# One quarter of the first weight matrix through SyncE's queue, with its cast on VectorE

## The chip, the cores and the metric

The kernel runs on one core of a Trainium2 chip. The metric is device time in microseconds (us) for one launch. A core has five engines that each run their own instruction list in order: TensorE (PE in the profile, its weight loads PEld), VectorE (DVE), ScalarE (ACT), GpSimd (POOL) and SyncE (SP). Transfers between the chip's memory and the core are issued by SyncE, ScalarE or GpSimd, and are then carried out by 16 DMA engines that all queues share.

## The reference

Two functions in a row. The first is a causal convolution with 7 taps over time, one set of taps for each of 8 groups of 24 channels; the second is a two-layer network with a Swish whose steepness is a parameter for each hidden column.

```python
w = exp(weight - max(weight)); w = w / (sum(w) + 1e-9)         # weight: [8, 7]
out = einsum('hk,bskhg->bshg', w, windows_of_7(x))              # x: [8, 4096, 192]
h = out.reshape(32768, 192) @ w_in                              # w_in: [192, 2048]
g = h * (1 / (1 + exp(-beta * h)))                              # beta: [2048]
return (g @ w_out).astype(float32)                              # w_out: [2048, 192]
```

All inputs and the output are float32 in memory; the kernel multiplies in bf16 (the convolution of the first tile in fp32r).

## The kernel before

**Tiling.** The 32,768 tokens are cut into two streams of 16,384 (`NS = 2`), which lie in the two halves of the partitions. The 192 channels are cut in three (`NK = 3`), so that 64 partitions hold one third for one stream. A step i takes n tokens of each stream: 128, 128, 256 for i = 0, 1, 2, then larger ones up to 512. In a step, the first product (`mm1`, with `ph` as its PSUM tile) makes 128 hidden columns at a time, ScalarE applies the Swish (Silu with a scale), and the second product (`mm2`, into `po`) is run for the step before.

**The start.** Steps 0 to 2 are run apart, by `mm1_pair(i, u)` for u = 0 to 7. Call one such call (i, u). It multiplies two sets of 128 columns at once, number u and number u + 8: one from each half of `w_in`, with stream-independent weights in the two halves of the partitions. So (0, 0) and (0, 1) need columns 0 to 256 of each half, (0, 2) and (0, 3) columns 256 to 512, (0, 4) and (0, 5) columns 512 to 768, and (0, 6) and (0, 7) columns 768 to 1024. `ph` has two buffers: (i, u) can't begin until ScalarE has finished the call two before.

Between these calls, `first_tile(i, u)` places by hand the convolution of the first 512 tokens of each stream, four blocks of 128. For a block b, `transpose_0` (TensorE, L215) turns x; `take_0` (L223) copies the result from PSUM into `xr`; `conv_0` (L229) applies the taps as matmuls with diagonal weights, eight in its first part and six in its second; `evac_0` (L240 on VectorE) scales the two results into the `xcp` tiles that `mm1_pair` reads. Blocks 0 and 1 are turned before (0, 0). Blocks 2 and 3 (numbers from 0) are turned together at (0, 3). Block 1's convolution lies at (0, 1) and (0, 2), block 2's at (0, 5) and (0, 6), block 3's at (1, 0) and (1, 1). `scale_w_out` (L273), sixteen calls on VectorE, multiplies the rows of `w_out` by 1/beta; the first `mm2` calls (L374), from (1, 2) on, need them.

**Loading.** `w_in` is float32 in memory and wanted as bf16. `load_w_in` (L113) uses GpSimd's queue, whose transfers convert the type on the way. That queue carries, in this order:

```python
    for f0, f1 in ((0, 256), (256, 640), (640, HF)):      # HF = 1024, half of w_in
        for s in range(NS):
            load_w_in(s, HF * s + f0, HF * s + f1)
        if f0 == 256:
            for b in range(2, NB):
                load_x0(b, nc.gpsimd)                     # blocks 2 and 3 of x
```

After these eight transfers come four of `w_out` (L157), two for the next blocks of x (`xb1`, L159), two more of x (L81), and four `copy_w_in` (L116), which put each half of `w_in` also into the other half of the partitions, for step 3 on. The program makes the ninth and each later transfer of this queue wait until the one eight places before it has landed.

SyncE's queue carries only the taps, block 0 of stream 0, beta and block 1 of x before it comes to the transposes of step 3. All instructions of an engine keep the order in which the program writes them (`pin`).

Of the kernel before, what the change touches and what calls it, by code (L numbers as in the profile page):

```python
# [10 lines left out]
FP32 = mybir.dt.float32  # L11
# [8 lines left out]
def kernel(  # L20
# [9 lines left out]
    nc = tc.nc  # L30
# [7 lines left out]
    NK = 3  # L38
    Q = D // NK
    NS = 2  # L40
# [3 lines left out]
    NB = TILE // 128  # L44

    def pin(ins):

        return tc.keep_in_program_order(ins)
# [4 lines left out]
    consts = ctx.enter_context(tc.tile_pool(name="consts", bufs=1))  # L53
# [23 lines left out]
    def load_x(j, s, b0=0, b1=NB, eng=None):  # L77
        if j not in xf_of:
            xf_of[j] = xf_pool.tile([128, NB, NS, D], FP32, name="xf")
        src = xs[s, TILE * j + 128 * b0:TILE * j + 128 * b1, :]  # L80
        pin((eng or nc.sync).dma_start(out=xf_of[j][:, b0:b1, s, :],  # L81
                                       in_=src.rearrange("(b p) d -> p b d", p=128)))

    def cast_x(j, s, b0=0, b1=NB, eng=None):
        if j not in xbf_of:
            xbf_of[j] = xbf_pool.tile([128, NB, NK, NS, Q], BF16, name="xb")
        pin((eng or nc.vector).tensor_copy(  # L87
            xbf_of[j][:, b0:b1, :, s, :].rearrange("p b k q -> p k b q"),
            xf_of[j][:, b0:b1, s, :].rearrange("p b (q k) -> p k b q", k=NK)))

    def new_xt(j):
        xt_of[j] = xt_pool.tile([128, NK, LEAD + TILE], BF16, name="xt")

    def transpose_x(j, b):
        if j not in xt_of:
            new_xt(j)
        c = LEAD + 128 * b
        pin(nc.sync.dma_start_transpose(
            out=xt_of[j][:, :, c:c + 128],
            in_=xbf_of[j][:, b, :, :, :].rearrange("p k s q -> p (k s q)")))  # L100


    w_in_s = consts.tile([128, NK, F], BF16, name="w_in_s")
    w_in_v = moe_w_in.rearrange("(q k) f -> q k f", k=NK)
# [4 lines left out]
    def half_of(s):  # L109
        return slice(64 * s, 64 * s + 64)  # L110

    def load_w_in(s, f0, f1):
        pin(nc.gpsimd.dma_start(out=w_in_s[half_of(s), :, f0:f1], in_=w_in_v[:, :, f0:f1]))  # L113

    def copy_w_in(s, f0, f1):
        pin(nc.gpsimd.dma_start(out=w_in_s[half_of(1 - s), :, f0:f1], in_=w_in_s[half_of(s), :, f0:f1]))  # L116
# [3 lines left out]
    xb0 = consts.tile([128, 2, NS, D], BF16, name="xb0")  # L120
# [7 lines left out]
    HF = F // 2  # L128

    def load_x0(b, eng):  # L130
        pin(eng.dma_start(out=x0[:, b, :, :] if b < 2 else xb0[:, b - 2, :, :],  # L131
                          in_=xs[:, 128 * b:128 * b + 128, :].rearrange("s p d -> p s d")))

    load_x0(1, nc.sync)

    one = consts.tile([128, 1], FP32, name="one")
    pin(nc.vector.memset(one, 1.0))
# [9 lines left out]
                                pattern=[[0, NS], [-1, H], [0, Q // H]], channel_multiplier=1))  # L147
    pin(nc.gpsimd.affine_select(out=ident, in_=ident, compare_op=ALU.not_equal, fill=1.0,  # L148
                                base=0, pattern=[[-1, 128]], channel_multiplier=1))
    for f0, f1 in ((0, 256), (256, 640), (640, HF)):  # L150
        for s in range(NS):
            load_w_in(s, HF * s + f0, HF * s + f1)
        if f0 == 256:
            for b in range(2, NB):
                load_x0(b, nc.gpsimd)
    for c in range(0, NF, 4):
        pin(nc.gpsimd.dma_start(out=w_out_f[:, c:c + 4, :], in_=w_out_v[:, c:c + 4, :]))  # L157
    for s in range(NS):
        pin(nc.gpsimd.dma_start(out=xb1[:, :, s, :],  # L159
                                in_=xs[s, TILE:TILE + 256, :].rearrange("(b p) d -> p b d", p=128)))  # L160
# [12 lines left out]
    def po_banks():  # L173
        return [po_bank(), po_bank()]
# [34 lines left out]
    def transpose_0(bank, src, b):  # L209

        bf = src.dtype == BF16
        t = (bank.bitcast(BF16) if bf else bank)[:, 0:NK * 128].rearrange("p (k t) -> p k t", k=NK)
        v = src[:, b, :, :].rearrange("p s d -> p (s d)").rearrange("p (m k) -> p k m", k=NK)
        for kk in range(NK):
            pin(nc.tensor.transpose(t[:, kk, :], v[:, kk, :], ident_b if bf else ident))  # L215
        return t

    def take_0(t, b, act=False):
        dst = xr[:, :, PAD + 128 * b:PAD + 128 * b + 128]
        if act:  # L220
            pin(nc.scalar.activation(dst, t, AF.Copy))
        else:
            pin(nc.vector.tensor_copy(dst, t))  # L223

    def conv_0(cv, b, k0=0, k1=K):

        for k in range(k0, k1):
            for s in range(NS):
                pin(nc.tensor.matmul(  # L229
                    cv[s][:, 0:NK * 128], diag[half_of(s), k, :, :].rearrange("p s q -> p (s q)"),  # L230
                    xr[half_of(s), :, 128 * b + k:128 * b + k + 128], start=(k == 0), stop=(k == K - 1)))

    def evac_0(cv, b, s, eng, k0=0, k1=NK):
        i, c = place[b]
        src = cv[s][:, 128 * k0:128 * k1].rearrange("p (k t) -> p k t", t=128)
        dst = xc_of[i][:, s, k0:k1, c:c + 128]
        if eng is nc.scalar:
            pin(nc.scalar.activation(dst, src, AF.Copy, scale=rsum))
        else:
            pin(eng.tensor_scalar_mul(dst, src, rsum))  # L240

    new_xt(0)
    pa = po_banks()
    pb = po_banks()
# [4 lines left out]
        make_diag(k)  # L249
    rsum = consts.tile([128, 1], FP32, name="rsum")  # L250
    pin(nc.vector.reciprocal(rsum, tsum))
    for f in range(0, HF, 512):
        for s in range(NS):
            copy_w_in(s, HF * s + f, HF * s + f + 512)
    pin(nc.scalar.activation(scrap, one, AF.Silu))
    b0 = [cv0[:, 0, :], pb[0]]
    conv_0(b0, 0)
# [6 lines left out]
    beta = consts.tile([128, NF], FP32, name="beta")  # L264
    pin(nc.vector.tensor_copy(beta, beta_ps))
    take_0(t1, 1)
    rbeta = consts.tile([128, NF], FP32, name="rbeta")
    pin(nc.vector.reciprocal(rbeta, beta))
    tapn = consts.tile([128, K], FP32, name="tapn")
# [2 lines left out]
    def scale_w_out(c):  # L272
        pin(nc.vector.tensor_scalar_mul(w_out_s[:, c, :], w_out_f[:, c, :], rbeta[:, c:c + 1]))  # L273
# [225 lines left out]
    def first_tile(i, u):  # L499
        if (i, u) == (0, 1):  # L500
            conv_0(pb, 1, 0, 4)
        elif (i, u) == (0, 2):
            conv_0(pb, 1, 4, K)
        elif (i, u) == (0, 3):
            t23 = [transpose_0(pa[b], xb0, b) for b in range(2)]
            for b in range(2):
                take_0(t23[b], 2 + b)
            for s in range(NS):
                evac_0(pb, 1, s, nc.vector)
        elif (i, u) == (0, 5):  # L510
            conv_0(pa, 2, 0, 4)
            for c in range(4):
                scale_w_out(c)
        elif (i, u) == (0, 6):
            conv_0(pa, 2, 4, K)
            for s in range(NS):
                evac_0(pa, 2, s, nc.vector)
            for c in range(4, 8):
                scale_w_out(c)
        elif (i, u) == (1, 0):  # L520
            conv_0(pb, 3, 0, 4)
        elif (i, u) == (1, 1):
            conv_0(pb, 3, 4, K)
            for s in range(NS):
                evac_0(pb, 3, s, nc.vector)
            for c in range(8, NF):
                scale_w_out(c)
        elif (i, u) == (1, 6):
            new_xt(1)
            ts_ = [transpose_0(pb[b], xb1, b) for b in range(2)]  # L530
            for b in range(2):
                pin(nc.vector.tensor_copy(xt_of[1][:, :, LEAD + 128 * b:LEAD + 128 * b + 128], ts_[b]))
            pin(nc.vector.tensor_copy(xt_of[0][:, :, TILE + LEAD - PAD:],
                                      xr[:, :, TILE:].bitcast(FP32)))
        elif (i, u) == (1, 7):
            for s in range(NS):
                cast_x(1, s, 2, NB)
            for b in range(2, NB):
                transpose_x(1, b)
            for j in (2, 3):  # L540
                for s in range(NS):
                    load_x(j, s)
# [69 lines left out]
```

## Time and profile before

| What | Value |
|---|---|
| Median of four runs | 686.74 us (686.05 to 687.60) |
| The profiled execution, its own time | 686.78 us |
| Its span in the profile | 684.9 us |
| TensorE busy | 679.4 us (99% of the span) |
| ScalarE busy, VectorE busy | 584.8 us (85%), 551.1 us (80%) |
| Granted TensorE clock | 1.00 |

The profiled execution's own time is 1.9 us over its span, and it is 0.04 us over the median. Times below are counted from the span's start. Spans of a busy TensorE are modelled at their end, and consecutive ones overlap; the starts of instructions are what the text reads. In a timeline line the first number is the start, the second the length of the merged piece, and the bracket at its end tells how long the engine was idle before it and what ended that.

### The profile page before, as it was taken

The numbers are of one execution on the slowest core, as the hardware profiler recorded it, in microseconds if no ns is written. First come the engines' busy times: TensorE is split into PE (matmuls) and PEld (weight loads), VectorE is DVE, ScalarE is ACT, GpSimd is POOL, SyncE is SP. The second block draws the span as 40 slices with busy tenths as digits, with TensorE's granted clock in tenths as the row PEclk, the third lists the DMA queues.
The fourth block names the chain that finished last, engine by engine and source line by source line (L and its number), as shares of the span: only waits on it lengthen the run. The fifth ranks groups of instructions, "written<-read, shape, count | busy, mean of one in ns | idle before, by whom it ended". The sixth has DMA issues, their size and how long they took to land.

```text
span 684.9 us, 27204 instructions
## 1 busy us (share of the span) xinstructions
PE 679.4 (99%) x12528; PEld 460.4 (67%) x12528; DVE 551.1 (80%) x886; ACT 584.8 (85%) x585; POOL 14.5 (2%) x26
## 2 busy tenths in 40 slices
PE   9999999999999999999999999999999999999998
PEld 6799887666666666666666666666666666666667
DVE  5999999999988889878889888889878889875112
ACT  7999999888888888888888888888888888888881
POOL 7000000000000000000000000000000000000000
PEclk9999999999999999999999999999999999999999
DMA  9752444344422444523444323344324443220223
GB/s 193 195 138 85 124 109 118 83 117 117 118 71 66 109 109 117 116 55 84 106 112 117 103 53 99 100 118 117 94 49 106 105 117 72 59 57 5 49 48 94
DMA packets 150418, 66.85 MB, mean 98 GB/s; under 512 B 113648, under 2 KB 149696, under 8 KB 150304
## 3 DMA queue, kind: packets, MB, share of 16 engines
q1 hardware_dynamic: 146992, 61.08, 34.9%
q0 software_dynamic: 3168, 3.93, 2.8%
q8 instruction: 98, 1.61, 1.0%
q14 instruction: 16, 0.13, 0.1%
q10 hardware_dynamic: 144, 0.10, 0.0%
HBM read 28.32 MB, written 25.17 MB: 78 GB/s over the span
## 4 chain that ended last, share of the span: by engine, by line
PE 97%; DMA 1%; POOL 1%; ACT 1%; issue 0%; DVE 0%; POOLq 0%
PE ph L342 47%; PE po L420 43%; PE po L374 4%; PE po L458 2%; PE ph L325 1%; DMA w_in_s<-in_moe_w_in_dram 1%; ACT g L329 1%; POOL w_in_s L113 0%; PE po L229 0%; ACT gp L329 0%; POOL xb L131 0%; PE po L215 0%; POOL sel L146 0%; DVE o_sp L380 0%; POOL ident L148 0%
## 5 line engine op out<-in xcount | busy, mean ns | idle before, releaser
L346 ACT ACTIVATE g<-ph,beta 128x1024 bf16<-128x1024 f32 (+2 forms) x528 | 558.1, 1062 | 80.4 <-PE ph L342 62.3
L342 PE MATMUL ph<-xc,w_in_s 64*64 64x512 bf16 (+3 forms) x5952 | 617.6, 369 | 0.3 <-ACT g L329 0.3
L420 PE MATMUL po<-g,w_out_s 64*64 64x512 bf16 (+1 forms) x5568 | 580.9, 373 | 0.0
L342 PEld LDWEIGHTS <-w_in_s 64*64 64x64 bf16 (+1 forms) x5952 | 274.9, 104 | 125.6 <-issue 0.5
L420 PEld LDWEIGHTS <-w_out_s 64*64 64x64 bf16 x5568 | 290.4, 118 | 84.3
L303 DVE SCALAR_TENSOR_TENSOR acc<-xt,tapn,acc 128x512 f32<-128x512 bf16 (+2 forms) x450 | 311.0, 759 | 0.9
L437 DVE STREAM_TRANSPOSE o_sb<-po 128x512 f32<-128x512 f32 (+1 forms) x87 | 76.1, 875 | 112.3 <-PE po L420 112.2
L303 DVE SCALAR_TENSOR_TENSOR xc<-xt,tapn,acc 128x512 bf16<-128x512 bf16 (+2 forms) x90 | 63.9, 760 | 0.2
L87 DVE CAST xb<-xf 128x768 bf16<-128x768 f32 (+1 forms) x62 | 48.7, 822 | 0.0
L301 DVE TENSOR_SCALAR acc<-xt,tapn 128x512 f32<-128x512 bf16 (+2 forms) x90 | 40.9, 485 | 1.1
L374 PE MATMUL po<-w_out_s,g 64*128 64x192 bf16 x512 | 32.6, 243 | 0.0
L374 PEld LDWEIGHTS <-g 64*128 64x128 bf16 x512 | 24.9, 94 | 1.6
L325 PE MATMUL ph<-xcp,w_in_s 64*128 64x256 bf16 (+1 forms) x144 | 15.1, 307 | 1.1 <-DMA w_in_s<-in_moe_w_in_dram 0.8
L380 DVE COPY o_sp<-po 128x192 f32<-128x192 f32 x28 | 9.0, 352 | 8.4 <-PE po L458 7.3
L329 ACT ACTIVATE gp<-ph,beta 128x256 bf16<-128x256 f32 x32 | 12.7, 476 | 1.9 <-PE ph L325 1.5
L458 PEld LDWEIGHTS <-g 128*128 128x128 bf16 x128 | 10.5, 98 | 0.4 <-issue 0.4
L458 PE MATMUL po<-w_out_s,g 128*128 128x192 bf16 x128 | 10.7, 247 | 0.0
L325 PEld LDWEIGHTS <-w_in_s 64*128 64x128 bf16 x144 | 6.8, 94 | 4.6 <-issue 1.6
L329 ACT ACTIVATE g<-ph,beta 128x512 bf16<-128x512 f32 x16 | 9.6, 692 | 0.1
L374 PE MATMUL po<-w_out_s,gp 64*128 64x192 bf16 x128 | 7.6, 243 | 0.0
L229 PE MATMUL po<-xr,diag 64*128 64x384 f32 x49 | 7.0, 362 | 0.0
L374 PEld LDWEIGHTS <-gp 64*128 64x128 bf16 x128 | 6.0, 94 | 1.6
(52 smaller groups left out, 57.3 us busy)
## 6 DMA issues: line engine op xcount, KB each, us to landing
xf<-in_x_dram SPq DMA_DIRECT2D x60, 384.0 KB, 4.1
out_dram<-o_sb SPq DMA_DIRECT2D x108, 192.0 KB, 4.6
xt<-xb SPq DMA_TRANSPOSE x122, 2.4
out_dram<-o_sp SPq DMA_DIRECT2D x10, 192.0 KB, 3.4
w_out_f<-in_moe_w_out_dram POOLq DMA_DIRECT2D x4, 384.0 KB, 7.6
out_dram<-o_sb SPq DMA_DIRECT2D x8, 144.0 KB, 4.3
w_in_s<-w_in_s POOLq DMA_DIRECT2D x4, 192.0 KB, 6.5
out_dram<-o_sp SPq DMA_DIRECT2D x8, 96.0 KB, 1.9
```

The source lines that it names most:

```text
L87: pin((eng or nc.vector).tensor_copy(xbf_of[j][:, b0:b1, :, s, :].rearrange("p b k q -> p k b q"), xf_of[j][:, b0:b1, s, :].rearrange("p b ...
L301: pin(nc.vector.tensor_scalar_mul(a, src, w))
L303: pin(nc.vector.scalar_tensor_tensor(out=xc_of[i][:, k0:k1, o:o + m] if k == K - 1 else a, in0=src, scalar=w, in1=a, op0=ALU.mult, op1=ALU ...
L325: pin(nc.tensor.matmul(ph[:, h, 0:NS * n], w_in_s[half_of(h), kk, ts(fcs[h], 128)], xc_of[i][half_of(h), :, kk, :], start=(kk == 0), stop= ...
L329: pin(nc.scalar.activation(g_at(i, fcs[h])[:, :, 0:n], ph[:, h, 0:NS * n].rearrange("p (s t) -> p s t", s=NS), AF.Silu, scale=beta[:, fcs[ ...
L342: pin(nc.tensor.matmul(ph[m0:m1, s, 0:n], w_in_s[half_of(s), kk, 128 * fc + m0:128 * fc + m1], xc_of[i][half_of(s), kk, 0:n], start=(kk == ...
L346: pin(nc.scalar.activation(g_at(i, fc)[:, :, 0:n], ph[:, :, 0:n], AF.Silu, scale=beta[:, fc:fc + 1]))
L374: pin(nc.tensor.matmul(po[q][:, 0:D], g_at(i, fc)[r, s, ts(b, 128)], w_out_s[r, fc, :], start=(phase == 0 and fc == 0), stop=(phase == 1 a ...
L380: pin(nc.vector.tensor_copy(dst, po[:, 0:D]))
L420: pin(nc.tensor.matmul(po_of[i, m][half_of(s), 0:n], w_out_s[half_of(r), fc, m:D:NM], g_at(i, fc)[half_of(r), s, 0:n], start=(first and fc ...
L437: pin(nc.vector.transpose(osb_of[i][:, 0:n // L, :, m], po_of[i, m][:, 0:n].rearrange("p (b l) -> p b l", l=L)))
L458: pin(nc.tensor.matmul(po[:, 0:D], g_at(i, fc)[:, s, ts(b, 128)], w_out_s[:, fc, :], start=(fc == 0), stop=(fc == NF - 1)))
```

## The change

The columns 256 to 512 of each half of `w_in` no longer go through GpSimd's queue. SyncE loads them as float32 into a new tile `w_in_f`, two transfers issued behind block 1 of x, and VectorE casts them into `w_in_s` in four copies of 64 partitions by 3 x 128 elements. These stand on VectorE between `take_0` of block 1 and the reciprocal of beta. The four `copy_w_in` are written behind the casts, and the two that hold those columns wait for them.

GpSimd's queue now carries columns 0 to 256, then 512 to 768, then block 2 of x, then columns 768 to 1024, then block 3 of x: again eight transfers before `w_out`. Block 3 of x is turned at (0, 7) in place of (0, 3), into another PSUM bank, and is taken by VectorE there, behind block 2's `evac_0`. The first eight `scale_w_out` follow it, where before four stood at (0, 5) and four at (0, 6).

```diff
     load_x0(1, nc.sync)
+    W0, W1 = 256, 512
+    w_in_f = consts.tile([128, NK, W1 - W0], FP32, name="w_in_f")
+    for s in range(NS):
+        pin(nc.sync.dma_start(out=w_in_f[half_of(s), :, :], in_=w_in_v[:, :, HF * s + W0:HF * s + W1]))
...
-    for f0, f1 in ((0, 256), (256, 640), (640, HF)):
+    for f0, f1, b in ((0, W0, None), (W1, 768, 2), (768, HF, 3)):
         for s in range(NS):
             load_w_in(s, HF * s + f0, HF * s + f1)
-        if f0 == 256:
-            for b in range(2, NB):
-                load_x0(b, nc.gpsimd)
+        if b:
+            load_x0(b, nc.gpsimd)
...
-    for f in range(0, HF, 512):
-        for s in range(NS):
-            copy_w_in(s, HF * s + f, HF * s + f + 512)
...
     take_0(t1, 1)
+    for f in range(0, W1 - W0, 128):
+        for s in range(NS):
+            w = HF * s + W0 + f
+            pin(nc.vector.tensor_copy(w_in_s[half_of(s), :, w:w + 128], w_in_f[half_of(s), :, f:f + 128]))
+    for f in range(0, HF, 512):
+        for s in range(NS):
+            copy_w_in(s, HF * s + f, HF * s + f + 512)
...
         elif (i, u) == (0, 3):
-            t23 = [transpose_0(pa[b], xb0, b) for b in range(2)]
-            for b in range(2):
-                take_0(t23[b], 2 + b)
+            take_0(transpose_0(pa[0], xb0, 0), 2)
             for s in range(NS):
                 evac_0(pb, 1, s, nc.vector)
         elif (i, u) == (0, 5):
             conv_0(pa, 2, 0, 4)
-            for c in range(4):
-                scale_w_out(c)
         elif (i, u) == (0, 6):
             conv_0(pa, 2, 4, K)
             for s in range(NS):
                 evac_0(pa, 2, s, nc.vector)
-            for c in range(4, 8):
+        elif (i, u) == (0, 7):
+            take_0(transpose_0(pb[0], xb0, 1), 3)
+            for c in range(8):
                 scale_w_out(c)
```

## The prediction

> **What bounds the kernel now.** I read the page's busy times and chain first, then the waits of the first 32 us, then the timeline of each engine there, then the transfers one by one.
>
> ```profile
> PE 679.4 (99%) x12528; PEld 460.4 (67%) x12528; DVE 551.1 (80%) x886; ACT 584.8 (85%) x585; POOL 14.5 (2%) x26
> ...
> PE 97%; DMA 1%; POOL 1%; ACT 1%; issue 0%; DVE 0%; POOLq 0%
> ...
> PEld L325 <- DMA w_in_s<-in_moe_w_in_dram: 1.3, 2, 1.0
> ...
> PE ph L325 <- DMA w_in_s<-in_moe_w_in_dram: 0.8, 1, 0.8
> ```
>
> TensorE is the bound; the change touches none of its work after step 2. What there is to win is the 1% of the chain that is a transfer of `w_in` (the waits' columns: total us, times, longest). It lies here:
>
> ```profile
> 10.28 0.52 PE L215 MATMUL po<-ident_b,xb 128*128 128x128 bf16 x6
> 10.73 0.81 PE L325 MATMUL ph<-xcp,w_in_s 64*128 64x256 bf16 x7
> 12.37 0.39 PE L325 MATMUL ph<-xcp,w_in_s 64*128 64x256 bf16 x4 [0.82 <-DMA w_in_s<-in_moe_w_in_dram]
> ...
> 13.32 0.50 PE L325 MATMUL ph<-xcp,w_in_s 64*128 64x256 bf16 x5
> ...
> 15.09 0.97 PE L229 MATMUL po<-xr,diag 64*128 64x384 f32 x8
> 15.90 0.51 PE L325 MATMUL ph<-xcp,w_in_s 64*128 64x256 bf16 x6
> ```
> ```profile
> 10.74 1.02 DVE L223 CAST xr<-po 128x384 fp32r<-128x384 bf16 x2 [2.18 <-PE po L215]
> ...
> 14.42 1.13 DVE L240 TENSOR_SCALAR xcp<-po,rsum 128x384 bf16<-128x384 f32 x2
> 15.47 0.99 DVE L273 TENSOR_SCALAR w_out_s<-w_out_f,rbeta 128x192 bf16<-128x192 f32 x4
> 16.97 1.14 DVE L240 TENSOR_SCALAR xcp<-po,rsum 128x384 bf16<-128x384 f32 x2 [0.51 <-PE po L229]
> ```
>
> In the first of these two timelines (TensorE, VectorE), 10.73 is (0, 4); its seventh matmul, at about 11.2, is the first of (0, 5), which then stops for columns 640 to 768 until 12.37. (0, 6) begins at 13.32, (1, 1) at 15.90. The reader is to note what VectorE does behind (0, 6): block 2's two `evac_0` from 14.42 to 15.47, and only then other work. Block 3 has by then long been taken, at 10.74 to 11.7.
>
> The transfers' own answers (issue start and time to landing) give: columns 0 to 256 landed at 5.7 and 6.3, columns 256 to 640 at 7.1 and 8.3, blocks 2 and 3 of x at 8.8 and 9.3, columns 640 to 1024 at 11.2 and 12.3. Two of those waits end the stall. From 4.2 us on, the DMA engines are full (2 to 12 us, 40 slices of 0.25 us):
>
> ```profile
> DMA  7680147879999999999899999998999888999999
> ```
>
> **The change, part by part.**
>
> *The stall at (0, 5).* Its columns now come in the queue's second piece, and (0, 6) needs the third, columns 768 to 1024. Ahead of that third piece lie 24 packets per engine less of `w_in`, one x block less, but 24 packets of SyncE's on the same engines. Packets counted in stretches of the transfers' view and divided by 16 engines: a converting packet of 512 B (columns 0 to 256) took an engine about 45 ns, of 768 B (the later pieces) 68 ns, of an x block about 32 ns, SyncE's 768 B ones about 35 ns, so I take 45 ns for its new 1,024 B ones. At about 5.1 us, 11 packets per engine of the first piece are left. Before: 11x45 + 24x68 + 32x32 + 24x68 = 4.8 us, so 9.9 on a mean engine, where 12.3 was the last landing: the slowest engine lags by 2.4. After: 11x45 + 24x45 + 16x32 + 24x45 + 24x45 (SyncE's) = 4.2 us, so 9.3, with the same lag 11.7 (estimates). (0, 5) can't begin before ScalarE is done with (0, 3), at 10.76 + 0.47 = 11.23; then 0.26 to its convolution and 0.81 for that (15.09 to 15.90) put (0, 6) at 12.30. So the piece is in time by 0.6 us, the stall is gone, and (0, 6) begins 1.02 us earlier (13.32 to 12.30).
>
> *What is late next: `take_0` of block 3.* It was at (0, 3); it now stands on VectorE behind block 2's two `evac_0`, and the convolution at (1, 0) waits for it. From the trace: (0, 6) to the first `evac_0` 1.10 us (13.32 to 14.42), the two 1.05 (14.42 to 15.47), the take 0.55 (one of 128x384 from PSUM, at 7.54), to the convolution 0.05, the convolution's first part 0.81, then (1, 1). That is 12.30 + 3.56 = 15.86, where (1, 1) began at 15.90. TensorE, which keeps its order, stands about 0.9 us at (1, 0) in place of (0, 5). Of 1.02 us won, 0.04 is left.
>
> *The three transposes taken out at (0, 3)* (0.23 us of TensorE) are put back at (0, 7), both beside a TensorE that waits for ScalarE or VectorE: nothing.
>
> *`scale_w_out`.* Its first eight calls at 0.247 us (0.99 for four) run from 14.96 (0.51 behind the take's start, as between the two takes at 10.74) to 16.94; block 3's `evac_0` was started by TensorE at 16.97. The first three are wanted by `mm2` at 17.1 and are done by 15.7. `w_out`'s first two transfers landed at 13.3 and 14.4. Nothing, by a margin of 0.03 us at block 3; behind that all stands as before, ScalarE being busy without a break from 17.33 to 31.75.
>
> *The four casts.* They fall into the 2.18 us in which VectorE waited (the bracket at 10.74), behind `take_0` of block 1, at 8.0. The nearest row is a cast of the same 384 elements, two in 0.90 us, one every 0.41:
>
> ```profile
> 21.11 0.90 DVE L87 CAST xb<-xf 128x384 bf16<-128x384 f32 x2
> ```
>
> At that price the first pair is done at 8.90 and the second at 9.7, in time for (0, 2) at 8.96 and (0, 3) at 9.84. [...] I take the row; the sum is the same by both, 0, as long as the data is there. The ends are 0 and, with the 0.49 of one cast alone, 0.15.
>
> *SyncE's two transfers.* Nothing else stands on SyncE's queue until 22 us, so no issue is delayed. They issue at about 2.5 and 2.9 and follow block 1 of x (3.9 us to landing, at 6.0). With its engines shared packet by packet, 24 x (45 + 45) ns from 5.1 gives 7.3 on a mean engine, and with the lag of 1 us that the second piece showed, 8.3 (estimate). The casts of stream-half 1 are wanted at 8.41. Ends: 7.0 (SyncE served first; no gain, the casts begin at 8.0), and 9.7 (GpSimd's packets served three to one). I take 0.1 us of delay at (0, 2), which goes to the end unchecked. The first piece shares too: 6.3 becomes about 6.9, wanted at 7.34; hidden by 0.4, and 0.3 of loss if SyncE goes first.
>
> *GpSimd's queue.* Eight transfers stand before `w_out` as before. The second of `xb1` and the next now wait for the third piece, the last x transfer for block 3: landings of about 11.7 and 12.4, where it waited until 12.6 before. Nothing. The `copy_w_in` issue at 13.6 and later, long after the casts.
>
> [...] The trace: seven scalings on VectorE, float32 from SBUF to SBUF, ran beside GpSimd's issue of two x transfers, which took 1.46 us; two more of that size, beside which VectorE was idle for the first half, took 1.46 too.
>
> ```profile
> 4.01 1.54 DVE L199 TENSOR_SCALAR diag<-ident,etap 128x128 fp32r<-128x128 f32 x7 [0.42 <-ACT etap L195]
> ...
> 4.32 1.46 POOL L131 DMA_DIRECT2D xb<-in_x_dram  x2
> ...
> 10.00 1.46 POOL L159 DMA_DIRECT2D xb<-in_x_dram  x2
> ```
>
> [...]
>
> **The sum.** Against the profiled execution's 686.78 us: -1.02 for the stall, +0.98 for the new wait, +0.1 for late `w_in_f`, 0 for the rest: 686.84, and 686.8 to 686.9 against the median of 686.74, which is 0.04 lower. I say 686.9.
>
> **The rivals.**
> 1. *The gain is kept.* If block 3 is taken in time, (1, 1) begins up to 1.0 us earlier, ScalarE's unbroken run with it, and the end too: 685.8. For it: ScalarE is fed from two buffers and may ride over part of the wait. Against: TensorE is in order, and the take stands behind two copies that can't begin until TensorE has finished block 2. `xb1`, which landed at about 19.5 for a use at 20.11, would also allow only half of it.
> 2. *`w_in_f` comes late (slower).* Place: the wait of VectorE's second cast, and (0, 2) behind it, one for one from a landing of 8.4 on. At 9.7 it costs 1.3, at 10.4 2.0: 688.1 to 688.8. For it: full engines, and a queue on which SyncE's packets came slowly at 3.4 to 4.0. Against: at 4.4 to 5.0 that queue moved more packets than GpSimd's.
> 3. *The load pieces of GpSimd's queue are not earlier.* If the lag of the slowest engine grows, the third piece lands at 12.8 or later and (0, 6) moves with it, and everything behind: +0.5 to +1.0, 687.3 to 687.8.
> 4. *The change doesn't do what it says*: the DMA engines are full, so a second queue moves the bytes no faster. True, but pieces are reordered, which is what the first part counts; it is part of the forecast.
>
> **How the numbers follow.** A measurement of this kernel can tell about 0.2% (1.37 us) from no change: faster is below 685.4, slower above 688.1. The forecast has 0.66, rival 1 0.10, rival 2 0.13, rival 3 0.11. The forecast and rival 3 lie within 0.2%, but for 0.05 of things that I don't see on the slow side. Rival 1 is within too, but for its far end (0.04). Two thirds of rival 2 are slower. That makes 0.04 faster, 0.82 within, 0.14 slower. The range from 685.9 to 688.1 leaves out the far half of rival 1 and the slower part.
>
> **What would show it.** Right: no wait of L325 for a transfer of `w_in` between 10 and 13; (0, 6) near 12.3; instead a wait of PE L229 for DVE `xr` of about 0.9 at 14.1; (1, 1) near 15.9; casts between 8.0 and 9.7 with no or little wait. Wrong: (1, 1) before 15.4 (rival 1); VectorE waiting for `w_in_f` at 8 and L325 for the casts (rival 2); a wait for `w_in_s` at (0, 6) (rival 3); or time that moves after 32 us, where I count nothing.

## The result and the profile after

| | before | changed |
|---|---|---|
| median | 686.73 us (61 runs, 685.90 to 687.60) | 687.95 us (41 runs, 687.18 to 688.64) |
| the profiled execution, and its span | 686.78, 684.9 us | 687.94, 686.2 us |

The ratio is 1.0018, with a 95% interval from 1.0014 to 1.0023: 1.2 us slower. The forecast was no measurable change, 686.9, with a range from 685.9 to 688.1, and it gave the late landing of `w_in_f` a chance of 0.13. The time lies in the range, but 1.1 us above the forecast's sum of 686.84. That it lies inside is luck: the range was wide, and what the traces below show is in good part that rival, not the sum.

The page and the waits of the first 32 us of the changed kernel (total us, times, longest):

```profile
PE 680.9 (99%) x12528; PEld 461.0 (67%) x12528; DVE 552.4 (81%) x890; ACT 584.6 (85%) x585; POOL 14.6 (2%) x26
...
PE 99%; ACT 1%; DVE 0%; issue 0%
```

```profile
PE po L232 <- DVE xr L226: 0.6, 1, 0.6
```

The transfer of `w_in` has gone from the chain and from TensorE's waits, and the wait of block 3's convolution for `take_0` has come, as forecast. But the timeline of TensorE shows a loss ahead of the first matmul that uses anything the change touches. These are matmuls of block 0's convolution in the changed kernel, and (0, 0), (0, 6), block 3's convolution and (1, 1):

```profile
5.93 0.52 PE L232 MATMUL ph<-xr,diag 64*128 64x384 f32 x1
...
6.25 0.52 PE L232 MATMUL ph<-xr,diag 64*128 64x384 f32 x1
...
8.72 0.85 PE L332 MATMUL ph<-xcp,w_in_s 64*128 64x256 bf16 x12
...
13.71 0.52 PE L332 MATMUL ph<-xcp,w_in_s 64*128 64x256 bf16 x6
...
16.45 0.98 PE L232 MATMUL po<-xr,diag 64*128 64x384 f32 x8 [0.62 <-DVE xr L226]
17.27 0.50 PE L332 MATMUL ph<-xcp,w_in_s 64*128 64x256 bf16 x6
```

The same place before, and (0, 0):

```profile
5.81 0.34 PE L229 MATMUL ph<-xr,diag 64*128 64x384 f32 x1
...
5.99 0.33 PE L229 MATMUL ph<-xr,diag 64*128 64x384 f32 x1
...
7.34 0.94 PE L325 MATMUL ph<-xcp,w_in_s 64*128 64x256 bf16 x12
```

The matmuls follow one another by 0.32 us after, by 0.18 before: TensorE ran at little more than half its speed (below: half speed). In the trace's record of its clock, full speed begins at 5.26 us in the first profiled execution of before and at 8.82 in this one; below, the clock is said to open then. (The granted clock of 1.00 doesn't show it, because the record has no entry ahead of that time.) (0, 0) begins at 8.72 for 7.34, and (1, 1) at 17.27 for 15.90, 1.37 later. This looks as if the late clock were the whole loss. The runs below show that it is not: the changed kernel loses as much when its clock opens early.

### The profile page after: what moved, and what is told of

Its sections match the earlier page's. It is cut to its first block, busy times and chain, and to the rows that moved or that the text cites. A ratio compares the mean times of both kernels' runs of the same rounds, so it can differ in the third digit from the quotient of the medians.

```text
span 686.2 us, 27214 instructions
## 1 busy us (share of the span) xinstructions
PE 680.9 (99%) x12528; PEld 461.0 (67%) x12528; DVE 552.4 (81%) x890; ACT 584.6 (85%) x585; POOL 14.6 (2%) x26
## 4 chain that ended last, share of the span: by engine, by line
PE 99%; ACT 1%; DVE 0%; issue 0%
PE ph L349 47%; PE po L427 43%; PE po L381 4%; PE po L465 2%; PE ph L332 1%; PE po L232 1%; ACT g L336 1%; PE ph L187 0%; PE ph L232 0%; PE po L218 0%; ACT gp L336 0%; DVE xr L226 0%; PE ph L193 0%; DVE o_sp L387 0%; PE po L263 0%
## 5 line engine op out<-in xcount | busy, mean ns | idle before, releaser
L332 PE MATMUL ph<-xcp,w_in_s 64*128 64x256 bf16 (+1 forms) x144 | 14.5, 307 | 0.4 <-ACT gp L336 0.2
```

Of the source, the lines that this page charges most:

```text
L332: pin(nc.tensor.matmul(ph[:, h, 0:NS * n], w_in_s[half_of(h), kk, ts(fcs[h], 128)], xc_of[i][half_of(h), :, kk, :], start=(kk == 0), stop= ...
```

## The experiments

Each ratio is to the kernel before, with its 95% interval. The profile of a run is that of a single execution; what is read from it need not hold for every execution of that kernel.

### More filler matmuls

```diff
     warm(9, 256)
+    warm(1, 128)
...
-    warm(7, 128)
+    warm(8, 128)
```

> The changed kernel with 11 small filler matmuls before the first convolution where it has 10, one of them in a place where TensorE stood idle for taps, and one more behind the ninth large one (two more in all; they compute nothing that is used). Theory A (TensorE's clock was still half at 5.3 to 8.8 us, since the stretch before was just not busy enough, and that is the whole loss): full clock from about 5.3 us, (0,0) near 7.4, (1,1) near 15.9, and the time falls by 1.1 to 1.3 us against the changed kernel, to that of before. Theory B (the new transfers, which are in flight then, slow TensorE's reads): the first convolution stays at 0.32 us a pair and the time stays at 1.0018 of before. Theory C (when the clock opens is drawn anew in each execution or each program, whatever the activity): no telling, a mixture.

Measured: 688.23 us, 1.0022 (1.0014 to 1.0031). The clock opened at 8.98 in its profile (8.82 in the changed kernel's first), and TensorE's first convolution began 0.2 us later behind the added fillers. The loss isn't cured by a little more activity; theory A (a late clock is the whole loss, and a little activity mends it) is out in this form. The median lies 0.3 us above the changed kernel's.

### SyncE's transfers alone

```diff
     load_x0(1, nc.sync)
+    w_in_f = consts.tile([128, NK, W1 - W0], FP32, name="w_in_f")
+    for s in range(NS):
+        pin(nc.sync.dma_start(out=w_in_f[half_of(s), :, :], in_=w_in_v[:, :, HF * s + W0:HF * s + W1]))
```

> The kernel before with only SyncE's two float32 transfers of w_in added; nothing reads them. Theory A: with the matmuls unchanged the clock opens at 5.3 as before; the two transfers put 393 KB more in front of the late pieces of GpSimd's queue, so the stall at (0,5) grows by 0.8 to 1.2 us, ratio 1.0012 to 1.0018. Theory B: besides, the first convolution runs at 0.32 us a pair and (0,0) begins at 8.7; ratio 1.003 or more. Theory C: either clock.

Measured: 687.46 us, 1.0008 (1.0001 to 1.0014). The clock opened at 6.77 here, at neither of the two times, though TensorE's program is that of before. Block 0's convolution took 0.32 us a pair until then and 0.18 after, while SyncE's two transfers were in flight to 8.1 and 9.5: here half speed went with the clock, and theory B (slow reads) is out. The ratio lies under the expected 1.0012 to 1.0018, and the place was another: in this profile TensorE waited 0.29 us for GpSimd's second piece at (0, 2) and for none at (0, 5).

### Block 3 taken first

```diff
             conv_0(pa, 2, 4, K)
+            take_0(transpose_0(pb[0], xb0, 1), 3)
             for s in range(NS):
                 evac_0(pa, 2, s, nc.vector)
         elif (i, u) == (0, 7):
-            take_0(transpose_0(pb[0], xb0, 1), 3)
```

> The changed kernel with block 3 transposed and taken at (0,6), ahead of block 2's two copies out, so that the convolution at (1,0) need not wait for them. If the wait at (1,0) is what ate the gain of the stall: (1,1) comes 0.9 to 1.1 us earlier than in the changed kernel, and the time falls by as much, ratio to before about 1.0003, if the clock opens as late as in the changed kernel; 0.9985 if it opens early. If ScalarE, not that wait, sets the pace there: no change from 1.0018.

Measured: 687.65 us, 1.0015 (1.0008 to 1.0022); by the medians 0.3 us under the changed kernel where about 1 was expected. TensorE's timeline in its profile, (0, 6), (1, 1) and a wait behind (1, 4):

```profile
13.57 0.50 PE L332 MATMUL ph<-xcp,w_in_s 64*128 64x256 bf16 x6
...
16.36 0.50 PE L332 MATMUL ph<-xcp,w_in_s 64*128 64x256 bf16 x6
...
19.73 0.26 PE L381 MATMUL po<-w_out_s,gp 64*128 64x192 bf16 x2 [0.38 <-DVE w_out_s L280]
```

From (0, 6) to (1, 1) it takes 2.79 us, where the changed kernel took 3.56: the wait was real, and 0.77 of it is saved. Behind it VectorE has no room left: the ninth scaling of `w_out` now comes late, and `mm2` waits 0.38 for it. The wait at (1, 0) is partly handed on to the next one. In this profile, with the clock opening at 6.40, VectorE also waited 0.50 us for `w_in_f` between its first and second cast.

### The moved block alone

Here the kernel before has the edits at (0, 3) and (0, 5) to (0, 7) only.

```diff
         elif (i, u) == (0, 3):
-            t23 = [transpose_0(pa[b], xb0, b) for b in range(2)]
-            for b in range(2):
-                take_0(t23[b], 2 + b)
+            take_0(transpose_0(pa[0], xb0, 0), 2)
...
+        elif (i, u) == (0, 7):
+            take_0(transpose_0(pb[0], xb0, 1), 3)
+            for c in range(8):
+                scale_w_out(c)
```

> The kernel before with only the second part of the change: block 3 turned and taken at (0,7) and the first eight scalings behind it; all loads as before. By the prediction's own steps the stall at (0,5) stays and the wait at (1,0) comes on top: (1,1) about 0.98 us later, at 16.9, ratio 1.0014. Theory A: with the matmuls before 5 us unchanged the clock opens at 5.3. If the late clock comes with the moved block: (0,0) at 8.7 and ratio 1.003.

Measured: 687.54 us, 1.0010 (1.0004 to 1.0017). The clock opened at 4.84. TensorE's timeline, (0, 6) and (1, 1):

```profile
12.83 0.50 PE L325 MATMUL ph<-xcp,w_in_s 64*128 64x256 bf16 x5
...
15.56 0.98 PE L229 MATMUL po<-xr,diag 64*128 64x384 f32 x8 [0.55 <-DVE xr L223]
16.39 0.50 PE L325 MATMUL ph<-xcp,w_in_s 64*128 64x256 bf16 x6
```

3.56 us from the one to the other, the sum of the prediction to the hundredth, where before took 2.58. Here the stall at (0, 5) ended 0.5 us earlier than in the first profile of before (11.87 for 12.37), since its piece landed earlier, and with that (1, 1) came 0.49 late, not 0.98. The ratio is under the expected 1.0014, which its interval includes.

### One more profile of each kernel

No edit; one profiled execution each.

> The changed kernel as it is, one more look at it. If the clock's opening is a matter of the execution and not of the kernel, it opens at another time than 8.8; if it opens before 5.5, VectorE's second cast waits for w_in_f until about 9.4 and (0,2) begins at 9.9 or later, where 8.96 was its start before. If it opens near 8.8 again, nothing new.

> The kernel before as it is, one more look at it. If the clock's opening varies from execution to execution, it opens at another time than 5.3; if it opens late (6.4 to 9), the wait for w_in at (0,5) is shorter than the 0.8 to 1.1 us of the first look, and (0,6) still begins between 13.3 and 13.7.

The changed kernel took 687.96 us, as in its first profile (687.94), with the clock at full speed from 4.46 us. TensorE's timeline and VectorE's:

```profile
6.85 0.61 PE L218 MATMUL po<-ident,x 128*128 128x128 f32 x3 [0.31 <-DMA x<-in_x_dram]
...
7.55 0.83 PE L332 MATMUL ph<-xcp,w_in_s 64*128 64x256 bf16 x12
...
10.14 0.39 PE L332 MATMUL ph<-xcp,w_in_s 64*128 64x256 bf16 x4 [0.69 <-DVE w_in_s L270]
...
13.74 0.50 PE L332 MATMUL ph<-xcp,w_in_s 64*128 64x256 bf16 x6
...
17.29 0.50 PE L332 MATMUL ph<-xcp,w_in_s 64*128 64x256 bf16 x6
```

```profile
8.34 0.48 DVE L270 CAST w_in_s<-w_in_f 64x384 bf16<-64x384 f32 x1
9.66 1.55 DVE L270 CAST w_in_s<-w_in_f 64x384 bf16<-64x384 f32 x3 [0.83 <-DMA w_in_f<-in_moe_w_in_dram]
```

(0, 0) begins at 7.55, but the second cast can't start before SyncE's second transfer has landed, at 9.63, and (0, 2) stops for it until 10.14. (1, 1) then begins at 17.29: the same, within 0.02 us, as in the profile whose clock opened 4.4 us later. Late data and late clock lie beside each other, and either alone brings (0, 6) to the same place, 13.74 here and 13.71 there. The data was late for the forecast in both: that transfer landed at 9.63 and 9.59, where 8.3 was estimated.

The kernel before took 687.33 us with the clock at full speed only from 8.96. TensorE's timeline, (0, 0), (0, 4) with (0, 5), the start of (0, 6), and (1, 1):

```profile
8.72 0.93 PE L325 MATMUL ph<-xcp,w_in_s 64*128 64x256 bf16 x12
...
12.11 1.05 PE L325 MATMUL ph<-xcp,w_in_s 64*128 64x256 bf16 x12
...
13.83 0.28 PE L325 MATMUL ph<-xcp,w_in_s 64*128 64x256 bf16 x1
...
16.48 0.53 PE L325 MATMUL ph<-xcp,w_in_s 64*128 64x256 bf16 x6
```

(0, 0) is 1.38 us behind the first profile, exactly as in the first profile of the changed kernel. But (0, 5) runs straight on behind (0, 4), with no wait for `w_in`, and (1, 1) is only 0.58 behind, the time 0.55 (687.33 to 686.78). (0, 6), at 13.83, is 0.13 later than expected. The stall that the change takes out swallowed 0.8 us of a late clock. So both kernels are in part blind to the clock, for different reasons, and the first two profiles happened to have an early one before and a late one after.

Set beside each other with a late clock in both (this profile and the first of the changed kernel), (0, 6) begins at 13.83 before and 13.71 after, and (1, 1) at 16.48 and 17.27. There nothing waits for `w_in_f`: the loss of 0.79 us is the wait for `take_0` of block 3, whose price is paid while no stall is left to win.

### The kernel before without the fillers

The kernel before without the nine large and seven small fillers.

```diff
-    warm(9, 256)
...
-    warm(7, 128)
```

> The kernel before without the nine large and the seven small filler matmuls ahead of the first convolution; [...] (0,0) begins at 8.5 or later, 1.2 us or more behind. Theory A (the stall for the third piece at (0,5) hides an early delay of up to 1.1 us): TensorE waits less or not at all for w_in at (0,5), and the time rises by only 0.1 to 0.6 us: ratio 1.0002 to 1.0009. If nothing is hidden: 1.2 to 1.8 us, ratio 1.0018 to 1.0026.

Measured: 687.39 us, 1.0006 (0.9999 to 1.0012). The clock opened at 8.61, (0, 0) began at 8.40, 0.1 us before the expected 8.5, and only TensorE's weight load still waited for `w_in`, 0.2 us: of a delay of 1.06 us about half reaches the end (0.54 by the medians, but the interval includes no change).

### Casts that don't wait for w_in_f

```diff
-            pin(nc.vector.tensor_copy(w_in_s[half_of(s), :, w:w + 128], w_in_f[half_of(s), :, f:f + 128]))
+            x384 = x0[half_of(s), 0, :, :].rearrange("p s d -> p (s d)").rearrange("p (k f) -> p k f", k=NK)
+            pin(nc.vector.tensor_copy(w_in_s[half_of(s), :, w:w + 128], x384))
```

> The changed kernel whose four casts read block 0 of x, which is there from 3.5 us on, in place of w_in_f; so those columns of w_in hold other numbers. All transfers stay. Theory A (late landing: with SyncE's second transfer landing at 9.3 to 9.5 us, the second cast and (0,2) can't begin before about 9.9, which is 1 us late, whatever TensorE's clock does): VectorE no longer waits at the casts, and the runs spread with the clock's opening, from about 687.0 to 688.1, median 0.2 to 0.6 us under the changed kernel's. Theory B (only the late clock makes the loss): same median as the changed kernel, 687.9 to 688.0.

Measured: 687.76 us, 1.0015 (1.0008 to 1.0022). The runs spread from 687.07 to 688.52, eight of 17 at or under 687.56; only two of the changed kernel's 41 lie under 687.6. These lower runs are what the late landing (theory A here) leads one to expect. But the median is only 0.2 us down, and these casts are not the same: the four took 2.27 us, where those from `w_in_f` took 1.80, and that puts about 0.5 us on the path ((0, 6) begins at 14.20 for 13.71). The profile had a clock opening of 9.16. The run supports the late landing and doesn't size it.

The same without the fillers, as above:

> Both edits: the casts read block 0 of x (those columns of w_in hold other numbers), and the sixteen filler matmuls are gone[...]. Here no transfer is waited for, so a late clock goes to the end: against the kernel whose casts read block 0 of x but keeps the fillers, +0.6 to +1.2 us by theory A, where the kernel before with the same cut loses 0.1 to 0.6. If the two lose the same, the stall hid nothing.

Measured: 688.15 us, 1.0023 (1.0014 to 1.0032), all ten runs between 688.03 and 688.54. Against the same kernel with fillers that is +0.39, and the kernel before lost 0.54 without them (687.39 against 686.85, measured beside it). The expectation missed. A comparison of medians can hardly carry it, since many executions with fillers have a late clock too (after 8 us in four of the ten profiles with unchanged fillers). What agrees is that the lower runs are gone.

### SyncE's loads in the order of the casts

```diff
-    for s in range(NS):
-        pin(nc.sync.dma_start(out=w_in_f[half_of(s), :, :], in_=w_in_v[:, :, HF * s + W0:HF * s + W1]))
+    for f in range(0, W1 - W0, 128):
+        for s in range(NS):
+            w = HF * s + W0 + f
+            pin(nc.sync.dma_start(out=w_in_f[half_of(s), :, f:f + 128], in_=w_in_v[:, :, w:w + 128]))
```

> The changed kernel with SyncE's two transfers cut into four of 128 columns, in the order in which the casts want them (both halves' columns 256 to 384 first). If late w_in_f sets the pace: the first two land at about 8.3, the casts for (0,2) no longer wait for 9.5, and the time falls by 0.2 to 0.6 us, ratio 1.0009 to 1.0015. If the clock alone, or the load of the engines as such, sets it: 1.0018 as before, or more by the smaller packets.

Measured: 687.86 us, 1.0011 (1.0005 to 1.0018). The ratio is as expected; the median is only 0.1 us under the changed kernel's. The runs may show why: 687.07 to 687.40 (seven of 21), where the changed kernel has one in 41, and a pack at 687.86 to 688.04, which it has too. The reading is that with earlier data the runs with an early clock gain up to 0.9 us, those with a late one nothing. The profile had the clock at 9.65, the first two loads landing at 7.6 and 8.4, and no wait of VectorE at the casts. That the groups are those of the clock is argued from single profiles; no run shows clock and time for a whole group.

Both edits that gained, together: the take of block 3 first and the split loads, each with the diff shown above.

> The changed kernel with both edits that gained something: SyncE's loads in four parts in the order of the casts, and block 3 taken ahead of block 2's copies out. If the two gains lie at different places they add up where the clock opens early: lowest runs at 686.5 to 686.9, where the split alone has 687.1; where it opens late, 687.4 to 687.6. Median 687.0 to 687.3, ratio 1.0003 to 1.0008: near the kernel before, not below it. If VectorE is full by then, no more than the split alone, 1.0011.

Measured: 687.20 us, 1.0007 (0.9999 to 1.0016), 686.79 to 687.66. By the ratios the gains add up: from 1.0018, 0.0003 for the take, 0.0007 for the loads, 0.0011 for both, with intervals that overlap. The median is 0.75 us under the changed kernel's and still 0.5 above that of before, measured beside it (686.66). In its profile, with the clock opening at 6.98, (0, 3) was served late by the casts, and `mm2` waited 0.35 for the ninth scaling: VectorE, with about 2 us of casts more, is short of time at both places. No version here beats the kernel before.

## Why the prediction was right or wrong

- **The stall at (0, 5) goes: right.** No profile of the changed kernel or of its variants has a wait of TensorE for GpSimd's pieces of `w_in`. The third piece landed at 10.9 and 11.1 in the first profile, before my 11.7.
- **What is late next: right, and to the size.** (0, 6) to (1, 1), forecast 3.56: 3.56, 3.55 and, with the move alone, 3.56. So a price of about 1 us is paid in each of these profiles.
- **`scale_w_out`: right.** Eight scalings from 16.31 took 1.95 us and ended when block 3's copies out were wanted. That VectorE had no room behind it showed as soon as one edit made TensorE earlier. (I put the landing of `w_out`'s second transfer in before at 14.4; it was 14.5, which changes nothing.)
- **The casts: right in price**, 0.45 us each (four in 1.80), as in the row I took, and hidden only as long as the data is there. GpSimd's issues hardly changed beside them: two of `w_out` took 0.82 and 0.75 us there, and in before, with no casts, 0.76 each (four in 3.04).
- **SyncE's two transfers: the step that failed.** I had the landing at 8.3 and 0.1 us of delay; it landed at 9.6 in both profiles, and with an early clock the second cast began at 9.66 in place of 8.41. The price was about right, one for one from 8.4 (rival 2: 688.1 for a landing at 9.7), and the landing was 1.3 us off. I let SyncE's packets begin at 5.1 and cost 90 ns with their partners, which ends at 7.3, and added 1 us of lag; in the trace the packets began at 5.2, the last one ended at 8.75, and the landing was 0.84 us after that. So 8.3 was 0.45 us short of the last packet, and the lag of 1 us, read from GpSimd's second piece, didn't cover the 0.84 us behind it. Why those took so long stays open.
- **Block 1 of x: a cost that I set to nothing.** I used its 3.9 us to landing as if the new transfers behind it left it alone. It took 4.7, landed at 6.8, and TensorE waited 0.31 us for it where the clock was early; (0, 0) began 0.21 late. The first piece of `w_in` landed at 7.3, where I had 6.9. In five profiles with SyncE's loads block 1 took 4.5 to 4.9 us, and in before and with the move alone 3.9 and 3.8: it was later by 0.6 to 1.1 us though it stood ahead of the new transfers in its queue.
- **The sum.** In the profile with the early clock: +0.21 for block 1, and the late casts then make (0, 6) begin at 13.74 for a forecast 12.30, (1, 1) at 17.29 for 15.86. That is 1.43, where I had 0.1. The price of the move was to be paid by an earlier (0, 6), and in no profile with SyncE's loads did (0, 6) begin before 13.31 (13.32 in before): late data held it where the clock was early, a late clock where it was not. How the 1.2 us of the medians divides between the two isn't shown.
- **What I did not see at all: the clock.** I took one profiled execution with an early clock for the kernel. That before hides more than half of a late one behind its stall, and would lose this when the stall goes, was in none of my cases; in the changed kernel a late clock cost nothing more, since the data alone was as late.

## What to carry to other kernels

The engines that move data were full here (nine tenths busy or more in 36 of 40 slices from 4 to 10 us before, in 37 after), and a second queue didn't bring its columns sooner (they landed at 8.3 and 9.6, for 7.1 and 8.3 before) but took from what was in flight (block 1 of x landed 0.8 us later, `w_in`'s first piece 1.0). In such a case work out the landing of every transfer that shares the time, also of those ahead of it in its queue, and add the lag of the slowest engine and the time from the last packet to the landing (0.84 us here). A stall also hides things; before you count on taking it away, ask which other delays, such as a late clock or a busy copier, stand behind it at nearly the same length. Take more than one profile of a start-up phase, and read the spread of the runs, before you call a difference there a cause.

## What the runs showed of the hardware

The time from which TensorE ran at full speed changed from execution to execution, with the same matmuls up to there: 5.26 and 8.96 us in two profiles of before, 8.82 and 4.46 in two of the changed kernel, and between 4.84 and 9.65 in six others with unchanged fillers. In the first profiles of both kernels the record has one stretch at full speed of the same length, 679.25 us, though it begins at 5.26 in one and at 8.82 in the other. None of the ten openings lies between 5.26 and 6.40 us. What decides the time, no run here shows: the sixteen fillers don't settle it, since the clock opened at 8.61 without them and in four of the ten profiles with them after 8 us too. At half speed the first convolution took 0.32 us a pair for 0.18, and (0, 0) began 1.38 us later (8.72 for 7.34).
